# The up product of eight half blocks in seven products instead of eight, on one core

## The chip, the cores and the metric

The kernel runs on one core of one Trainium2 chip. The metric is the device time of one launch in microseconds (us), the median of several runs. A profiled execution is read beside it; its span leaves out a little of what the device time counts (731.9 us against 733.69 us for the same execution).

Five engines work side by side: TensorE (PE in the profile, with its weight loads as PEld), VectorE (DVE), ScalarE (ACT), GpSimd (POOL) and SyncE (SP, which only issues transfers here).

## The reference

Retention over a sequence, then two matrix products with an activation between them, all in f32:

```python
B, H, S, D = 4, 8, 768, 64
for t in range(S):
    state = gamma * state + k[:, :, t] (outer) v[:, :, t]
    y[:, :, t] = scale * q[:, :, t] @ state
x = y.transpose(0, 2, 1, 3).reshape(B * S, H * D)      # 3072 x 512
h = x @ w_in                                           # 512 x 2048   "up"
g = h - np.tanh(h)
out = g @ w_out                                        # 2048 x 512   "down"
```

## The kernel before

The 3072 tokens are 24 chunks of 128. Four chunks make a block, two chunks a half block of 256 tokens: n = 0 to 11. The 2048 inner columns are eight pairs of 128, m2 = 0 to 7. One step (n, m2) makes the up product of one half block and one pair, its activation, and (two steps behind, LAG) the down product of an earlier step. There are 96 steps. The last eight half blocks (n = 4 to 11) run one after the other, eight steps each. Attention work for the later chunks is spread over the steps in between; it ends in half block 5.

The up product is eight matmuls of 256 columns into one bank of PSUM (the matrix engine's accumulator):

```python
def up(n, m2, i):                       # called for i = 0, 1
    if i == 0:
        hps[n, m2] = bank("h", f"h_{n}_{m2}")           # 128 x 512 f32, two of them in turn
    hp = hps[n, m2][:, ts(i, TH)]                       # TH = 256
    for c in range(NC):                                 # NC = 4
        nc.tensor.matmul(hp, w1[:, c, ts(2 * m2 + i, P)], xT[n // 2][:, c, ts(n % 2, TH)],
                         start=(i == 0 and c == 0), stop=(c == NC - 1), ...)
```

The activation (h - tanh h, with a polynomial where h is small) takes five ACT and six DVE instructions over 128x512:

```python
u  = Square(hp);  th = Tanh(hp)                                            # ACT, L429, L430
q0 = Square(u + ..); q1 = Square(sqrt(A) u + ..); large = Relu(u - 0.5)    # ACT, L437 to L439
th = hp - th                                                               # DVE, L445
hp = (R - u) * hp                                                          # DVE, L446
hp = (q0 + C0) * hp                                                        # DVE, L448
hp = (q1 + A * C1) * hp                                                    # DVE, L454
g  = hp * u                                                                # DVE, L458
copy_predicated(g, large, th)                                              # DVE, L459
```

The down product of half blocks 5 to 11 is done in seven matmuls of 256 columns instead of eight (2x2 blocks by the Strassen-Winograd scheme). GpSimd makes four sums of g for it (128x128 each, L545 to L548) and, once, 16 sums of w_out (128x512 each, L536). The seven results lie in four banks, and DVE adds them up at the end of a half block:

```python
def fast_down(n, m2, first, last):
    ...
    for k in (1, 2, 4, 6, 7, 5, 3):
        nc.tensor.matmul(accs[n][k], left[k - 1], right, ...)       # L581

def fast_end(n):                        # after m2 = 7
    nc.scalar.copy(out=p1, in_=acc[1])
    # seven DVE additions of 128x256 in one burst (L597, L599), two transfers out
```

The loop over the steps, with attention and weight conversion cut:

```python
for s in range(BEGUN, len(steps)):
    ... # attention work in every second step, up to s = 45: PE, ACT, DVE, and the split of k, q
    ... # (turn_by_dma: ACT copies, a transfer out, a transposing transfer back)
    for i in range(2):
        up(n, m2, i)
    waiting.append(steps[s])
    shrink_begin(n, m2)                 # u, th
    shrink_factors(n, m2)               # q0, q1, large
    shrink_multiply(n, m2)              # three DVE operations
    downs(LAG)                          # the down product of two steps before
    shrink_end(n, m2)                   # three DVE operations
    if n >= FAST:
        fast_sums(n, m2)                # POOL
```

Of the kernel before, what the change touches and what calls it, by code (L numbers as in the profile page):

```python
# [9 lines left out]
F32 = mybir.dt.float32  # L10
# [3 lines left out]
AF = mybir.ActivationFunctionType  # L14
ALU = mybir.AluOpType

P = 128
# [15 lines left out]
def kernel(  # L33
# [7 lines left out]
    tables: bass.AP,  # L41
    out: bass.AP,
):

# [265 lines left out]
    def mask(ci):  # L312
        halves = scores[ci]
        m = mid.tile([P, 2, NP, D], F32, tag="a", name=f"a_{ci}")
        nc.vector.tensor_tensor(m, halves[:, :, 0],
                                causal[:, None, None, :].to_broadcast([P, 2, NP, D]),
                                op=ALU.mult)
        masked[ci] = m
# [70 lines left out]
    def outputs_rest(ci):  # L389
        halfway.pop(ci)(False)  # L390
        loaded.pop(ci)
# [18 lines left out]
    def work(tag, bufs):  # L410
        return tmp.tile([P, BANK], F32, tag=tag, name=tag, bufs=bufs)
# [14 lines left out]
    def shrink_begin(n, m2):  # L426
        hp = hps[n, m2]
        u, th = (work(x, 2) for x in ("u", "th"))
        nc.scalar.activation(u, hp, AF.Square)  # L429
        nc.scalar.activation(th, hp, AF.Tanh)  # L430
        shrinking[n, m2] = [u, th]

    def shrink_factors(n, m2):
        u = shrinking[n, m2][0]
        large = work("large", 2)
        q0, q1 = (work(x, 1) for x in ("q0", "q1"))
        nc.scalar.activation(q0, u, AF.Square, bias=bias0)  # L437
        nc.scalar.activation(q1, u, AF.Square, bias=bias1, scale=math.sqrt(A))  # L438
        nc.scalar.activation(large, u, AF.Relu, bias=bias_m)  # L439
        shrinking[n, m2] += [q0, q1, large]  # L440

    def shrink_multiply(n, m2):
        hp = hps[n, m2]
        u, th, q0 = shrinking[n, m2][:3]
        nc.vector.tensor_tensor(th, hp, th, op=ALU.subtract)  # L445
        nc.vector.scalar_tensor_tensor(hp, in0=u, scalar=R, in1=hp, op0=ALU.subtract,  # L446
                                       op1=ALU.mult, reverse0=True)
        nc.vector.scalar_tensor_tensor(hp, in0=q0, scalar=C0, in1=hp, op0=ALU.add,  # L448
                                       op1=ALU.mult)

    def shrink_end(n, m2):
        hp = hps.pop((n, m2))
        u, th, _, q1, large = shrinking.pop((n, m2))
        nc.vector.scalar_tensor_tensor(hp, in0=q1, scalar=A * C1, in1=hp, op0=ALU.add,  # L454
                                       op1=ALU.mult)
        g = gp.tile([P, 2, TH], F32, tag="g", name=f"g_{n}_{m2}")
        flat = g.rearrange("p i t -> p (i t)")
        nc.vector.tensor_tensor(flat, hp, u, op=ALU.mult)  # L458
        nc.vector.copy_predicated(flat, large.bitcast(I32), th)  # L459
        gT[n, m2] = g  # L460

    def down(n, m2, j, first, last):

# [22 lines left out]
    def rows_of(n):  # L486

        return out[ds(n * TH, TH)].rearrange("(p two) c -> p two c", two=2)
# [19 lines left out]

    FAST = 5
    PAIRS = NM // 2  # L510
    room = []
    t_of = {}

    def quarter(i, c, at):
        return w2[:, i::2, ts(c, TH)][:, ds(2 * at, 2)]

    def fast_weights(k, at):

        if not room:
            for _ in range(3):  # L520
                raw = stage.tile([P, 2, 2, TH], F32, tag="raw", name="fast_raw", bufs=3)
                room.extend(raw[:, i] for i in range(2))
            for tag in ("head", "low", "power"):
                room.extend(stage.tile([P, 2, TH], F32, tag=tag, name=f"fast_{tag}")
                            for _ in range(2))
        if k == 3 and at == 0:
            late = xp.tile([P, 4, 2, TH], F32, tag="xT", name="fast_x")
            room.extend(late[:, i] for i in range(4))
        t = t_of[k, at] = room[PAIRS // 2 * k + at]
        a, b = (  # L530
            (quarter(0, 1, at), quarter(0, 0, at)),
            (quarter(1, 1, at), t_of.get((0, at))),
            (quarter(1, 1, at), quarter(0, 1, at)),
            (t_of.get((1, at)), quarter(1, 0, at)),
        )[k]
        nc.gpsimd.tensor_tensor(t, a, b, op=ALU.subtract)  # L536

    fast_g = {}

# [28 lines left out]
        right = {2: 1, 7: 1, 4: 1, 6: n % 2}  # L568
        accs[n] = {k: b[:, ts(right.get(k, 0), TH)] for k, b in acc.items()}

    def fast_down(n, m2, first, last):
        if first:
            fast_banks(n)
        left = fast_g.pop((n, m2))
        for k in (1, 2, 4, 6, 7, 5, 3):
            right = (
                w2[:, 2 * m2, :TH], w2[:, 2 * m2 + 1, :TH], w2[:, 2 * m2 + 1, TH:],
                *(t_of[x, m2 // 2][:, m2 % 2] for x in (3, 0, 1, 2)),
            )[k - 1]

            nc.tensor.matmul(accs[n][k], left[k - 1], right, start=first and k in (1, 6, 7, 4),  # L581
                             stop=last, skip_group_check=True)

    def fast_end(n):
        acc = accs.pop(n)
        o = op.tile([P, 2, DM], F32, tag="sum", name=f"sum_{n}")
        c11, c12, c21, c22 = (o[:, j, ts(c, TH)] for j in range(2) for c in range(2))
        some = [mid.tile([P, 2, TH], F32, tag="a", name=f"fast_{n}") for _ in range(2)]
        p1, v_, x_, w_ = (t[:, i] for t in some for i in range(2))
        nc.scalar.copy(out=p1, in_=acc[1])  # L590
        add, sub = ALU.add, ALU.subtract
        for dst, k, b, how in (
            (c11, 2, p1, add), (v_, 6, p1, add), (w_, 7, v_, add), (c22, 5, w_, add),
            (x_, 5, v_, add), (c21, 4, w_, sub), (c12, 3, x_, add),
        ):
            if how is sub:
                nc.vector.tensor_tensor(dst, b, acc[k], op=sub)  # L597
            else:
                nc.vector.tensor_tensor(dst, acc[k], b, op=add)  # L599
            if dst is c21:  # L600
                nc.sync.dma_start(out=rows_of(n)[:, 1], in_=o[:, 1])
        nc.sync.dma_start(out=rows_of(n)[:, 0], in_=o[:, 0])

    waiting = []

    def part(j, n, m2, first, last):
        down(n, m2, j, first, last)
        if last:
            add_up(n, m2, j)

    def downs(lag):
        while len(waiting) > lag:
            tile_ = waiting.pop(0)
            if tile_[0] >= FAST:
                fast_down(*tile_)
                if tile_[3]:
                    fast_end(tile_[0])
                continue
            for j in range(2):
                part(j, *tile_)  # L620

# [4 lines left out]
    def tall(ci):  # L628
# [23 lines left out]
        "a": lambda s: shrink_begin(*steps[s][:2]),  # L652
        "q": lambda s: shrink_factors(*steps[s][:2]),
        "d": lambda s: shrink_multiply(*steps[s][:2]),
        "g": lambda s: shrink_end(*steps[s][:2]),
        "o": lambda s: [down(*steps[s][:2], j, *steps[s][2:]) for j in range(2)],
        "E": lambda s: [add_up(*steps[s][:2], j) for j in range(2)],
        "x": lambda n: idle.__setitem__(0, n),
# [17 lines left out]


    FIRST = 8
    LAST_WEIGHTS = NW - 6
    with_chunk = {BEGUN + 2 * i + 1: FIRST - 3 + i for i in range(NCH - FIRST + 3)}  # L680
    with_weights = {BEGUN: [12, 13]}
    for i in range(14, NW):
        with_weights[i - 5] = [i]
    fast_parts = [(k, at) for at in range(PAIRS // 2) for k in range(3)]
    fast_parts += [(3, at) for at in range(PAIRS // 2)]

    for s in range(BEGUN, len(steps)):
        n, m2, first, last = steps[s]
        ci = with_chunk.get(s)
        if ci is not None:  # L690
            if ci >= FIRST:
                outputs_rest(ci)
                keep_x(ci)
            if FIRST <= ci + 2 < NCH:
                products(ci + 2)
                mask(ci + 2)
                state(ci + 2)
            load_chunk(ci + 4)
            if ci + 3 < NCH:
                turn_by_dma(ci + 3)  # L700
            if FIRST <= ci + 1 < NCH - 1:
                outputs(ci + 1)
                see(ci + 1)
        for i in with_weights.get(s, []):
            convert(i)
            load_weights(i + 3)
        for i in range(2):
            up(n, m2, i)
        if ci == NCH - 2:
            outputs(ci + 1)  # L710
            see(ci + 1)
        waiting.append(steps[s])
        shrink_begin(n, m2)
        shrink_factors(n, m2)
        shrink_multiply(n, m2)
        downs(LAG)
        shrink_end(n, m2)
        if n >= FAST:
            fast_sums(n, m2)
        if s + 1 in with_chunk:  # L720
            for which in range(2):
                scale(with_chunk[s + 1] + 3, which, nc.gpsimd)
        if s > LAST_WEIGHTS + 1:
            for _ in range(min(2, len(fast_parts))):
                fast_weights(*fast_parts.pop(0))
    downs(0)


def _tables(H, D, S=768):
# [51 lines left out]
```

## Time and profile before

| | |
|---|---|
| device time, median of 3 | 734.24 us (733.23 to 734.8) |
| profiled span | 731.9 us, mean granted TensorE clock 0.997 |
| up matmuls (L420), 128x256, records | 1536, mean 381 ns |
| down matmuls by plain products (L468), 128x512, records | 320, mean 593 ns |
| GpSimd sums of g, 128x128 | 456 ns each |
| GpSimd sums of w_out (L536), 128x512 | 1.27 to 1.51 us each |
| DVE operations of the activation, 128x512 | 0.685 to 0.774 us each |

How to read it: matmuls are pipelined, so the mean of a record is longer than the distance from one to the next; the distance of starts counts. Busy shares are averages over the span. The chain that ended last follows the work back from the last instruction.

The last stretch has the same pattern for over 250 us. In five windows of 52 us from 448 to 708 us, PE is busy for 52.00 us in each, DVE for about 35.4, ACT for 23.56 and POOL for 13.94.

### The profile page before, as it was taken

How to read it: one execution, taken by the hardware profiler on the slowest of the kernel's cores; microseconds unless marked ns; L12 is line 12 of the kernel's file. 1: busy time of each engine (PE TensorE's matmuls, PEld its weight loads, DVE VectorE, ACT ScalarE, POOL GpSimd, SP SyncE). 2: the span in 40 equal slices, each digit the busy share in tenths (PEclk: the TensorE clock that was granted, in tenths of full speed). 3: DMA queues.
4: the chain of work that ended last, by engine and by line, in shares of the span. 5: the costliest groups of instructions: out<-in, count | busy, mean ns of one | idle time of the engine just before them, and what ended most of it. 6: DMA issues, size and time to landing. Idle time of an engine off the chain costs nothing.

```text
span 731.9 us, 14885 instructions
## 1 busy us (share of the span) xinstructions
PE 717.7 (98%) x5806; PEld 566.9 (77%) x5806; DVE 533.6 (73%) x849; ACT 389.7 (53%) x749; POOL 247.6 (34%) x348
## 2 busy tenths in 40 slices
PE   8899999999999999999999999999999999999996
PEld 7686666666776676677688888888888888888885
DVE  4999988998888777765566676676766766766764
ACT  4567557766777645565445444444444444444441
POOL 0565434544554555411012222222132222222221
PEclk9999999999999999999999999999999999999998
DMA  9883428776776566444100000000000000000000
GB/s 202 211 207 84 130 69 218 173 197 171 188 192 165 110 147 165 131 106 122 36 30 1 1 29 2 1 29 1 29 1 1 30 0 1 30 0 1 30 0 30
DMA packets 125399, 59.84 MB, mean 82 GB/s; under 512 B 109840, under 2 KB 118160, under 8 KB 125328
## 3 DMA queue, kind: packets, MB, share of 16 engines
q1 hardware_dynamic: 122880, 50.34, 28.4%
q10 hardware_dynamic: 2448, 8.54, 3.1%
q8 instruction: 46, 0.75, 0.4%
q14 instruction: 25, 0.20, 0.1%
HBM read 35.80 MB, written 14.68 MB: 69 GB/s over the span
## 4 chain that ended last, share of the span: by engine, by line
PE 91%; DMA 4%; DVE 2%; POOL 1%; SPq 1%; ACT 1%; issue 0%; DVEq 0%; POOLq 0%; ACTq 0%
PE h L420 44%; PE o L468 17%; PE fast_t L581 8%; PE y L581 8%; PE fast_o L581 7%; PE y L356 3%; DMA kqT<-rows 1%; PE s L302 1%; PE s L308 1%; DMA raws<-in_moe_w_in_dram 1%; DMA k<-in_k_dram 1%; DMA q<-in_q_dram 1%; SPq L233 1%; PE kqTp L254 1%; DMA rows<-apart 1%; DVE head L189 0%
## 5 line engine op out<-in xcount | busy, mean ns | idle before, releaser
L420 PE MATMUL h<-xT,w 128*128 128x256 f32 x1536 | 349.9, 381 | 1.1 <-DVE w L203 1.1
L420 PEld LDWEIGHTS h<-xT,w 128*128 128x128 f32 x1536 | 289.7, 190 | 50.1 <-issue 10.0
L429 ACT ACTIVATE u<-h 128x512 f32<-128x512 f32 x96 | 57.3, 597 | 259.7 <-PE h L420 259.5
L445 DVE TENSOR_TENSOR th<-h,th 128x512 f32<-128x512 f32 x96 | 66.2, 689 | 132.3 <-ACT th L430 132.2
L468 PE MATMUL o<-w,g 128*128 128x512 f32 x320 | 144.2, 593 | 0.0
L545 POOL TENSOR_TENSOR s<-g 128x128 f32<-128x128 f32 x56 | 25.5, 455 | 286.7 <-DVE g L459 282.3
L468 PEld LDWEIGHTS o<-w,g 128*128 128x128 f32 x320 | 60.5, 190 | 59.5 <-issue 56.7
L459 DVE COPY_PREDICATED g<-large,th 128x512 f32<-128x512 int32 x96 | 74.3, 774 | 9.8 <-DVE g L458 0.5
L448 DVE SCALAR_TENSOR_TENSOR h<-q,h 128x512 f32<-128x512 f32 x96 | 66.8, 696 | 10.0
L199 POOL TENSOR_TENSOR low<-low,power 128x512 f32<-128x512 f32 x30 | 38.6, 1288 | 102.4 <-DVE power L191 62.8
L454 DVE SCALAR_TENSOR_TENSOR h<-q,h 128x512 f32<-128x512 f32 x96 | 66.6, 694 | 8.9 <-DVE h L448 0.9
L458 DVE TENSOR_TENSOR g<-h,u 128x512 f32<-128x512 f32 x96 | 66.4, 692 | 6.9
L437 ACT ACTIVATE q<-u,tab 128x512 f32<-128x512 f32 x96 | 69.5, 724 | 0.0
L438 ACT ACTIVATE q<-u,tab 128x512 f32<-128x512 f32 x96 | 69.1, 720 | 0.0
L439 ACT ACTIVATE large<-u,tab 128x512 f32<-128x512 f32 x96 | 68.8, 716 | 0.0
L446 DVE SCALAR_TENSOR_TENSOR h<-u,h 128x512 f32<-128x512 f32 x96 | 65.8, 685 | 0.0
L430 ACT ACTIVATE th<-h 128x512 f32<-128x512 f32 x96 | 56.8, 591 | 0.0
L240 POOL TENSOR_TENSOR q<-q,tab 128x512 f32<-128x512 f32 x22 | 24.2, 1099 | 77.2 <-DMA q<-in_q_dram 52.0
L203 POOL TENSOR_TENSOR w<-low,head 128x512 f32<-128x512 f32 x30 | 38.5, 1284 | 2.4
L240 POOL TENSOR_TENSOR v<-v,tab 128x512 f32<-128x512 f32 x22 | 28.2, 1284 | 3.3 <-DMA v<-in_v_dram 3.3
L356 PEld LDWEIGHTS y<-a,v 64*64 64x64 f32 x768 | 15.9, 134 | 14.9 <-ACT large L439 10.9
L546 POOL TENSOR_TENSOR s<-s,g 128x128 f32<-128x128 f32 x56 | 25.6, 457 | 4.4
(110 smaller groups left out, 868.7 us busy)
## 6 DMA issues: line engine op xcount, KB each, us to landing
rows<-apart ACTq DMA_DIRECT2D x16, 512.0 KB, 4.4
k<-in_k_dram SPq DMA_DIRECT2D x24, 256.0 KB, 4.7
q<-in_q_dram SPq DMA_DIRECT2D x24, 256.0 KB, 5.1
v<-in_v_dram SPq DMA_DIRECT2D x24, 256.0 KB, 5.5
raw<-in_moe_w_out_dram SPq DMA_DIRECT2D x12, 512.0 KB, 4.1
out_dram<-sum SPq DMA_DIRECT2D x24, 256.0 KB, 2.3
raw<-in_moe_w_in_dram SPq DMA_DIRECT2D x14, 256.0 KB, 4.4
raw<-in_moe_w_in_dram SPq DMA_DIRECT2D x28, 128.0 KB, 4.2
```

The costliest lines, as they stand in the source:

```text
L420: nc.tensor.matmul(hp, w1[:, c, ts(2 * m2 + i, P)], xT[n // 2][:, c, ts(n % 2, TH)], start=(i == 0 and c == 0), stop=(c == NC - 1), skip_g ...
L437: nc.scalar.activation(q0, u, AF.Square, bias=bias0)
L438: nc.scalar.activation(q1, u, AF.Square, bias=bias1, scale=math.sqrt(A))
L439: nc.scalar.activation(large, u, AF.Relu, bias=bias_m)
L445: nc.vector.tensor_tensor(th, hp, th, op=ALU.subtract)
L446: nc.vector.scalar_tensor_tensor(hp, in0=u, scalar=R, in1=hp, op0=ALU.subtract, op1=ALU.mult, reverse0=True)
L448: nc.vector.scalar_tensor_tensor(hp, in0=q0, scalar=C0, in1=hp, op0=ALU.add, op1=ALU.mult)
L454: nc.vector.scalar_tensor_tensor(hp, in0=q1, scalar=A * C1, in1=hp, op0=ALU.add, op1=ALU.mult)
L458: nc.vector.tensor_tensor(flat, hp, u, op=ALU.mult)
L459: nc.vector.copy_predicated(flat, large.bitcast(I32), th)
L468: nc.tensor.matmul(o_p[j], gT[n, m2][:, i, ts(j, P)], w2[:, 2 * m2 + i], start=(first and i == 0), stop=(last and i == 1))
L581: nc.tensor.matmul(accs[n][k], left[k - 1], right, start=first and k in (1, 6, 7, 4), stop=last, skip_group_check=True)
```

## The change

The up product of half blocks 4 to 11 is done in seven products instead of eight, by the same 2x2 scheme as the down product: the blocks are 128 inner columns by 256 rows of w_in, and 256 rows by 128 tokens of x. A product is now two matmuls of 128 columns, so a step has 14 of them in place of eight of 256 columns. GpSimd makes the sums: four of 128x256 for each pair of w_in (once), four of 128x256 for each half block of tokens.

The seven results are put together partly by accumulation in PSUM. Four products (1, 5, 7, 6) go into the four quarters of a bank; ACT copies the bank to SBUF; GpSimd adds two pairs of quarters (P1 + P6, P5 + P7); the other three products (2, 3, 4) accumulate on the first three quarters; DVE adds the pairs where they are still missing.

```diff
+    def fast_up(n, m2, some):
+        if 1 in some:
+            hps[n, m2] = bank("h", f"h_{n}_{m2}")
+        for k in some:
+            for c in range(2):
+                nc.tensor.matmul(hps[n, m2][:, ts(PLACE[k], P)], s_of[m2][k - 1][:, c],
+                                 x_of[n][k - 1][:, c], start=(k == 1 and c == 0), stop=(c == 1),
+                                 skip_group_check=True)
+
+    def up_take(n, m2):
+        nc.scalar.copy(out=odd_room[0], in_=hps[n, m2])
+
+    def up_pairs():
+
+        first = odd_room[0].rearrange("p (i t) -> p i t", i=4)
+        nc.gpsimd.tensor_tensor(odd_room[1], first[:, :2], first[:, 3:1:-1], op=ALU.add)
+
+    def up_add(n, m2):
+        hp = hps[n, m2].rearrange("p (i t) -> p i t", i=4)
+        u, w = (odd_room[1][:, i] for i in range(2))
+        nc.vector.tensor_tensor(hp[:, 1:3], hp[:, 1:3],
+                                u[:, None, :].to_broadcast([P, 2, P]), op=ALU.add)
+        nc.vector.tensor_tensor(hp[:, 3], u, w, op=ALU.add)
```

The sums, one call a pair (`up_weights`) or a half block (`up_tokens`), with their tiles cut:

```diff
+        for k, x, y, how in ((3, a11, a21, ALU.subtract), (1, a21, a22, ALU.add),
+                             (2, s_[1], a11, ALU.subtract), (4, a12, s_[2], ALU.subtract)):
+            nc.gpsimd.tensor_tensor(s_[k], x, y, op=how)
...
+        for dst, a, b in ((t1, b12, b11), (t2, b22, t1), (t3, b22, b12), (t4, b21, t2)):
+            nc.gpsimd.tensor_tensor(dst, a, b, op=ALU.subtract)
...
+    for m2 in range(PAIRS):
+        with_sums.setdefault(FIRST_UP - 4 + m2, []).append(lambda m2=m2: up_weights(m2))
+        with_sums.setdefault(FIRST_DOWN + m2, []).append(lambda m2=m2: fast_weights(m2))
```

The sums of w_out for the down product are now four of 128x256 for each pair, made in the eight steps of half block 5 (`fast_weights` above), where the kernel before made 16 of 128x512 earlier.

The order within a step changes so that PE has other work while the results of its first four products are carried on. The down product is cut into its first four and its last three matmuls, and it now belongs to the step three before (one more than before). A tile's last factor, its multiplication and its predicated copy move into the next step. The last factor writes g in SBUF, so that the bank is free earlier:

```diff
+        if fast:
+            fast_up(n, m2, (1, 5, 7, 6))
+            up_take(n, m2)
...
+            if before and ci is None:
+                shrink_factors(*before)              # q1, large of the tile before
+                shrink_last_factor(*before)
+            up_pairs()
+            for make in with_sums.get(s, []):
+                make()
+            downs(lag, 0)                            # first four down matmuls
+            fast_up(n, m2, (2, 3, 4))
+            up_add(n, m2)
+            shrink_begin(n, m2)                      # th, then u
+            if before:
+                shrink_end(*before)                  # multiplication, predicated copy
+                if before[0] >= FAST:
+                    fast_sums(*before)
+            downs(lag, 1)                            # last three down matmuls
+            end_some(1)
+            shrink_two(n, m2)
+            before = n, m2
+            if s + 1 not in with_chunk:
+                middle()                             # q0 and the third factor
```

(The comments in this extract are added.) The additions at the end of a half block no longer come as one burst: two of the seven are issued at once, the other five one by one in the following steps (`end_some`):

```diff
+        add(c11, 2, p1)
+        add(v_, 6, p1)
+        for args in ((w_, 7, v_), (c22, 5, w_), (x_, 5, v_), (c21, 4, w_, True), (c12, 3, x_)):
+            ending.append(lambda args=args: add(*args))
```

In steps with attention work, the squares of the tile before (q0, q1, large) now stand in ACT's queue ahead of the copies that split k and q for their transposing transfer:

```diff
+        middle()
+        if before:
+            shrink_factors(*before)
+            shrink_last_factor(*before)
         if FIRST <= ci + 2 < NCH:
             products(ci + 2)
...
+        if not before:
+            turn_and_see(ci)                         # else after the first four up products
```

## The prediction

> **What bounds the kernel now.** I read the page's totals first, then the 40 slices, then the chain that ended last, and then one step of the last stage by engine.
>
> ```profile
> span 731.9 us, 14885 instructions
> ...
> PE 717.7 (98%) x5806; PEld 566.9 (77%) x5806; DVE 533.6 (73%) x849; ACT 389.7 (53%) x749; POOL 247.6 (34%) x348
> ...
> PE   8899999999999999999999999999999999999996
> ...
> PE 91%; DMA 4%; DVE 2%; POOL 1%; SPq 1%; ACT 1%; issue 0%; DVEq 0%; POOLq 0%; ACTq 0%
> ```
>
> TensorE (PE) is busy in every slice and carries 91% of the chain. A busy PE is only modelled, so the next view, matmuls in order of time, checks it: are there holes between the matmuls of two steps?
>
> ```profile
> 505.57 0.59 PE L581 MATMUL y<-w,s 128*128 128x256 f32 x2
> 506.00 3.62 PE L420 MATMUL h<-xT,w 128*128 128x256 f32 x16
> 509.45 1.03 PE L581 MATMUL fast_t<-w,g 128*128 128x256 f32 x4
> ...
> 512.04 0.59 PE L581 MATMUL y<-w,s 128*128 128x256 f32 x2
> 512.47 0.81 PE L420 MATMUL h<-xT,w 128*128 128x256 f32 x3
> ```
>
> One f32 matmul of the program is two records. The 16 records of the up product run from 506.00 to 509.45, 0.2157 us each, and a whole step from 506.00 to 512.47: 6.47 us = 30 records (16 up, 14 down) x 0.2157. No hole: the step is exactly its matmuls, and only fewer PE microseconds can shorten it, as long as no other engine then needs more than the new step.
>
> **What the new matmuls cost.** The change replaces 256-column up matmuls by 128-column ones, each with its own weight load. The kernel before has such a stream already, in the filler that keeps the array busy early on:
>
> ```profile
> 30.95 2.13 PE L216 MATMUL kqTp<-busy 128*128 128x128 f32 x17 [1.83 <-DVE state L331]
> 31.03 1.98 PEld L216 LDWEIGHTS kqTp<-busy 128*128 128x128 f32 x17
> ```
>
> The weight loads take 0.190 us as records, but their starts are (1.98 - 0.19) / 16 = 0.112 us apart: the load overlaps. So a 128-column record costs 0.112, which is 52% of 0.2157, not exactly half.
>
> The Trainium skill bears in three places. "TensorE: Matmul & The Clock Gate", section "LDWEIGHTS (loading the stationary operand)", puts a load of 128 columns at 128/1.2 = 107 ns; 112 ns between starts agrees, and it means that the load just fits under a 128-column matmul. "FP8 and Floating Point Precision", section "TensorE Precision Notes", says that true FP32 takes four passes; the two records per matmul, each about twice 128 or 256 columns long, fit that. "SBUF — State Buffer", section "SBUF: two separate sides", says that VectorE (DVE) instructions with two SBUF inputs and GpSimd (POOL) instructions lock each other out of a shared port for a whole instruction. The trace agrees: here a 0.74 us predicated copy (both inputs in SBUF) took 1.50 beside POOL's subtractions, one of which grew from 1.27 to 1.74, while DVE's operations on PSUM did not grow.
>
> ```profile
> 290.34 1.50 DVE L459 COPY_PREDICATED g<-large,th 128x512 f32<-128x512 int32 x1
> ...
> 289.96 1.27 POOL L536 TENSOR_TENSOR fast_head<-w,fast_raw 128x512 f32<-128x512 f32 x1
> 291.19 1.74 POOL L536 TENSOR_TENSOR fast_power<-w 128x512 f32<-128x512 f32 x1
> ```
>
> **The change, part by part.**
>
> PE. Half blocks 4 to 11 have 8 steps each: 64 steps. Up product before: 8 matmuls = 16 records x 0.2157 = 3.45 us. After: seven products of two 128-row pieces = 14 matmuls = 28 records x 0.112 = 3.14 us. Saved: 0.315 us a step, x 64 = 20.2 us. A pure step (half blocks 6 to 11, no attention work) goes from 6.47 to 3.14 + 3.02 = 6.16 us. The down product is only cut into four and three products, and the one extra tile of lag (a step without a down, and one down more at the end) moves 3.0 us from the middle to the tail without adding work.
>
> DVE. In a step of before its six operations start at 504.29, 504.90, 505.69, 506.49, 507.29 and 508.09: 0.61 us behind one they do not depend on, 0.80 behind one they do, 4.55 us in all. The change adds two additions of seven-product pieces: 128x256 at 0.42 us (as the sums of L599) and 128x128, by the slope (0.692 - 0.424) / 256 us per element about 0.28. It interleaves tiles, so some dependent pairs come apart. In the new order: last factor 0.61, additions 0.37 and 0.22, multiply 0.80, predicated copy 0.70, one output addition 0.35 (now one a step in five steps of eight, before a burst of seven), subtraction 0.61, two factors 0.80 + 0.80: 5.3 us of 6.16. It fits, with 0.9 us to spare where there were 1.9.
>
> ACT. Six operations of 0.5 to 0.6 us spacing instead of five: about 3.4 us of 6.16.
>
> POOL. The sums for the down product take 4 x 0.456 us and gaps, 2.0; new is one 128x256 addition, from 455 ns at 128 and 1274 at 512 elements about 0.73: 2.7 of 6.16. Token sums add 4 x 0.73 = 2.9 us once per half block. Weight sums add 2.9 us in each of eight steps around the start of half block 4 and again in the eight of half block 5 (the second lot replaces 16 subtractions of 1.3 to 1.5 us).
>
> **The path within a step.** With 0 at the first up matmul: the first four products, 16 records x 0.112, end at 1.8. ACT's copy of the bank (0.59 us, as its 128x512 copy of L268) can run from 2.0, with 0.2 for the array to drain and the signal, to 2.65. Four down matmuls, 8 x 0.2157 = 1.73, fill PE until 3.5; only then do the last three up products, which accumulate on what ACT has read, need that copy. Slack 0.75 us or more. They take 12 x 0.112 = 1.34 and end at 4.85; DVE's two additions run from 5.1 to 5.85; tanh, square and squared factor start 0.49, 0.48 and 0.61 us apart in the trace before, so ACT is done near 5.85 + 0.2 + 1.7 = 7.8 to 8.0, just ahead of the next copy at 6.16 + 2.0 = 8.2. DVE goes on from 5.85 through multiply, copy, output addition, subtraction and three factors, 0.8 + 0.7 + 0.45 + 0.61 + 3 x 0.8 = 5.0, to 10.9: then the bank is read out, and it is taken again two steps later at 12.3. So in pure steps no wait takes the place of the removed work; I expect 6.16 us, 48 x 0.315 = 15.1 us saved in half blocks 6 to 11.
>
> In half blocks 4 and 5 (5.0 us of the 20.2) I take losses off. In half block 5 POOL has 2.9 + 0.73 + 2.0 = 5.7 us a step, plus the time it waits for DVE's three operations with two SBUF inputs (0.28 + 0.8 + 0.74 = up to 1.8): 7.5 at worst, against steps of 6.2 without and about 8.3 with attention. That may cost some 2 to 3 us over the eight steps. Token sums and the first filling cost perhaps 0.5 us more.
>
> The tail: the last DVE chain (additions, the multiply and copy of the tile before, then six operations) ends about 12.1 us after the last step's start, and PE's remaining down products of three earlier tiles end at 12.2. It fits; afterwards, as before, one down, seven additions and the store.
>
> Sum: 734.2 - 20.2 + 2.5 = 716.5 us.
>
> **The rivals.**
>
> 1. DVE becomes the bound. Its spare 0.9 us a step rests on my counting of dependent and independent pairs. If all nine operations cost 0.1 more, the step is near 6.2 and nothing is lost; if the additions had to wait behind POOL each time, 0.7 more, the step returns to about 6.4 and only 5 us remain: some 729. For it: DVE goes from 4.55 to 5.3. Against: in pure steps POOL's sums run while DVE works on PSUM, where the trace shows no collision.
>
> 2. The new wait of PE on ACT's copy. Each step now has an exchange PE to ACT to PE, with 0.75 us to spare. A slip of the tile before by more than that shows up one to one on PE. For it: ACT's queue is in order, and the copy sits behind a square that depends on DVE's additions. If it cost 0.3 us in each of the 64 steps, all the gain would go: 734. Against: half the down product stands between, and is put there for that.
>
> 3. The weight load becomes the bound: with data other than one repeated tile, 128-column matmuls could be further apart than 0.112. At 0.123 us a record the seven products equal the eight. For it: only the early filler shows this form. Against: its loads are real loads, and PEld records keep 0.19 whatever they read.
>
> 4. Attention steps of half blocks 4 and 5 slow down, because ACT now does the shrink's squares ahead of the split of k, so that the transposing transfer starts later. It has 15 us until it is needed and takes 4.4 + 4.3 us; hidden.
>
> **Range and chances.** With nothing lost it is 714; with all of half block 5's gain and 0.05 us a pure step lost, about 719. Eight in ten: 712 to 724. Faster by over 2% means under 719.6, a saving of 14.7 of the possible 20.2: I give it 0.72. Within 2%: 0.23, mostly rivals 1 and 2. Slower by over 2% would need a real pile-up: 0.05.
>
> **What the profile after should show.** Right: step starts 6.16 us apart at 450 to 690; the new up line with 28 records a step, starts 0.112 apart; PE still full in all slices, PEld well above before; DVE near 85% there. Wrong: idle time on the up line's PE or PEld released by the ACT copy (rival 2); DVE without idle time and steps of 6.3 to 6.5 (rival 1); 128-column starts more than 0.115 apart (rival 3); long predicated copies beside POOL in half block 5 with steps above 7 there, more than I took off.

## The result and the profile after

| | before | after |
|---|---|---|
| device time, median of 4 | 733.83 us (733.23 to 734.8) | 717.15 us (716.57 to 718.03) |
| ratio, 95% interval | | 0.9773 (0.9756 to 0.9789) |
| profiled span | 731.9 us | 716.1 us |
| from the first seven-product matmul (287.88) or its counterpart (287.74) to the end | 444.2 us | 428.2 us |
| one half block of pure steps | 51.80 us | 49.23 us (half blocks 8 to 10), 49.86 (6 and 7) |

The last two rows take starts of matmuls from the traces. Ahead of that stretch TensorE's work is the same in both kernels; over all runs the stretch starts between 286.9 and 289.3 us.

The page of the changed kernel, its totals, slices and chain:

```profile
span 716.1 us, 16724 instructions
...
PE 699.4 (98%) x6574; PEld 573.4 (80%) x6574; DVE 579.1 (81%) x977; ACT 431.9 (60%) x813; POOL 347.6 (49%) x492
...
PE   8899999999999999999999999999999999999996
PEld 8676666667667776766779989989999999999995
DVE  4999988898898856788777888788788787887885
...
PE 85%; DVE 7%; ACT 3%; DMA 2%; POOL 1%; issue 1%; ACTq 0%; DVEq 0%; POOLq 0%
```

PE still leads. DVE and the weight loads have come up behind it, and the chain passes through DVE and ACT in places. One step of half block 9, all engines in order of time (start, duration, engine, line, output and inputs, count, idle before it):

```profile
583.95 0.61 PE L688 MATMUL h<-xT,w 128*128 128x128 f32 x4
584.40 0.61 PE L688 MATMUL h<-x,w 128*128 128x128 f32 x4
...
585.74 1.03 PE L616 MATMUL fast_o<-w,g 128*128 128x256 f32 x4
...
585.99 0.59 ACT L693 COPY fast_head<-h 128x512 f32<-128x512 f32 x1 [0.36 <-PE h L688]
...
587.25 0.63 PEld L688 LDWEIGHTS h<-xT,w 128*128 128x128 f32 x4
587.47 0.61 PE L688 MATMUL h<-xT,w 128*128 128x128 f32 x4
...
589.08 0.43 DVE L703 TENSOR_TENSOR h<-h,fast_head 128x256 f32<-128x256 f32 x1 [0.85 <-PE h L688]
...
590.10 0.61 PE L688 MATMUL h<-xT,w 128*128 128x128 f32 x4
```

Step to step: 590.10 - 583.95 = 6.15 us. Four 128-column records take 584.40 - 583.95 = 0.45, 0.112 each. ACT's copy ends at 586.58, 0.67 ahead of the weight load (587.25) and 0.89 ahead of the matmul (587.47) of the products that need it. DVE has waited 0.85 us for PE: it has time left, PE has none.

PE's longest waits in the last eight half blocks, in order of time, by matmuls:

```profile
304.55 0.71 PE L688 MATMUL h<-xT,w 128*128 128x128 f32 x4 [0.91 <-ACT fast_head L693]
...
309.81 0.69 PE L309 MATMUL s<-kqT 64*64 64x64 f32 x32 [1.07 <-DMA kqT<-rows]
...
425.91 0.67 PE L616 MATMUL fast_t<-fast_apart,g 128*128 128x256 f32 x2 [0.44 <-ACT q L448]
...
475.77 0.67 PE L616 MATMUL y<-fast_apart,g 128*128 128x256 f32 x2 [0.43 <-ACT q L448]
```

Counted from start to start, the lost times are larger than these idle times, because a pipelined matmul's record runs on: 1.07, 1.24, 0.68 and 0.68 us. The first two come behind the one step without a down product (the lag grows there, in half block 4). The last two stand in the first down step of half blocks 6 and 7. The square that is named as their releaser does not touch a bank of the down product, so something else held them (experiments 2 and 6).

### The profile page after: what moved, and what is told of

Read it like the earlier page. It is cut to its first block, busy times and chain, and to the rows that moved or that the text cites. A ratio compares the mean times of both kernels' runs of the same rounds, so it can differ in the third digit from the quotient of the medians.

```text
span 716.1 us, 16724 instructions
## 1 busy us (share of the span) xinstructions
PE 699.4 (98%) x6574; PEld 573.4 (80%) x6574; DVE 579.1 (81%) x977; ACT 431.9 (60%) x813; POOL 347.6 (49%) x492
## 4 chain that ended last, share of the span: by engine, by line
PE 85%; DVE 7%; ACT 3%; DMA 2%; POOL 1%; issue 1%; ACTq 0%; DVEq 0%; POOLq 0%
PE h L688 27%; PE o L490 16%; PE h L421 12%; PE fast_t L616 8%; PE y L616 8%; PE fast_o L616 7%; PE y L357 3%; DMA kqT<-rows 1%; PE s L309 1%; PE kqTp L217 1%; DVE head L190 1%; PE s L303 1%; DVE power L192 1%; DVE head L188 1%; PE kqTp L255 1%
## 5 line engine op out<-in xcount | busy, mean ns | idle before, releaser
L421 PE MATMUL h<-xT,w 128*128 128x256 f32 x512 | 117.7, 382 | 1.1 <-DVE w L204 1.1
L421 PEld LDWEIGHTS h<-xT,w 128*128 128x128 f32 x512 | 95.7, 190 | 20.9 <-issue 7.2
L688 PEld LDWEIGHTS h<-xT,w 128*128 128x128 f32 x512 | 76.2, 191 | 15.7 <-issue 7.1
L688 PE MATMUL h<-xT,w 128*128 128x128 f32 x512 | 78.9, 277 | 1.0 <-ACT fast_head L693 0.9
L465 DVE SCALAR_TENSOR_TENSOR h<-q,h 128x512 f32<-128x512 f32 x96 | 66.9, 696 | 11.5 <-ACT q L440 1.5
L703 DVE TENSOR_TENSOR h<-h,fast_head 128x256 f32<-128x256 f32 x64 | 27.6, 432 | 56.8 <-PE h L688 56.1
L698 POOL TENSOR_TENSOR fast_head<-fast_head 128x256 f32<-128x256 f32 x64 | 47.4, 740 | 46.1 <-ACT fast_head L693 34.5
L688 PE MATMUL h<-x,w 128*128 128x128 f32 x448 | 68.3, 275 | 0.0
L688 PEld LDWEIGHTS h<-x,w 128*128 128x128 f32 x448 | 59.0, 192 | 0.0
L693 ACT COPY fast_head<-h 128x512 f32<-128x512 f32 x64 | 37.5, 585 | 26.4 <-PE h L688 26.2
L474 DVE SCALAR_TENSOR_TENSOR g<-q,h 128x512 f32<-128x512 f32 x64 | 44.0, 687 | 7.8 <-ACT q L448 1.3
```

Of the source, the lines that this page charges most:

```text
L465: nc.vector.scalar_tensor_tensor(hp, in0=shrinking[n, m2][2], scalar=C0, in1=hp, op0=ALU.add, op1=ALU.mult)
L688: nc.tensor.matmul(hps[n, m2][:, ts(PLACE[k], P)], s_of[m2][k - 1][:, c], x_of[n][k - 1][:, c], start=(k == 1 and c == 0), stop=(c == 1), ...
L698: nc.gpsimd.tensor_tensor(odd_room[1], first[:, :2], first[:, 3:1:-1], op=ALU.add)
```

## The experiments

All times below are medians of timed runs beside the kernel before.

**1. The step without a down product, moved.** From the second step of half block 4 to the second step of half block 5.

```diff
-        falls_back = s == FIRST_UP + 1
-        lag = LAG + int(s >= FIRST_UP + 1)
+        falls_back = s == FIRST_UP + 9
+        lag = LAG + int(s >= FIRST_UP + 9)
```

> The step without a down product (where the lag grows from two tiles to three) moves from the second step of half block 4 to the second step of half block 5; nothing else changes. Theory A (PE runs ahead there because 3.45 us of down product are missing, so that ACT's copy and the transposed k and q come too late for it): the holes of 1.07 us (before the last three up products of the next step, waiting for ACT's copy) and of 1.24 us (before the products with the transposed k and q) in half block 4 go, and a hole of at most 1 us appears in half block 5, where no transposed k and q are due any more. Time 717.15 - 1.3 to 2.3 = 715 to 716. Theory B (the holes come from the new order of ACT's queue in attention steps, squares ahead of the split of k): both holes stay, time within 0.5 us of 717.

Measured: 714.75 us, ratio 0.974 (0.9724 to 0.9757). Both holes of half block 4 are gone. The products with the transposed k and q follow the ones ahead of them at once:

```profile
309.20 0.65 PE L303 MATMUL s<-v,k 64*64 64x64 f32 x32
309.67 0.65 PE L309 MATMUL s<-kqT 64*64 64x64 f32 x32
...
364.77 0.71 PE L688 MATMUL h<-xT,w 128*128 128x128 f32 x4 [0.18 <-ACT fast_head L693]
```

The last line is the new hole, 0.34 us from start to start. Theory A holds: PE ran ahead. (`falls_back` also puts that step's attention work behind its first four up products, and this moved along. Experiment 9 has neither and no such holes either, so no run separates the two.) From the first seven-product matmul to the end it is 425.9 us against 428.2, so 2.3 us; the rest of the gain in the profiled run lies in the stretch before.

**2. The token sums, two steps later.**

```diff
-        at_ = ... else PAIRS * (n - 1) + 2
+        at_ = ... else PAIRS * (n - 1) + 4
```

> GpSimd makes the token sums of half blocks 7 to 11 two steps later, away from the step in which the outputs of a half block are begun to be added up. Theory A (GpSimd's token sums hold DVE's two-SBUF-input operations up, so the first output additions come late, and the fourth down product of half blocks 6 and 7 waits for them): the two holes of 0.60 us plus 0.08 near 425 and 475 go, 717.15 - 1.3 = 715.8 us; the long multiplications of DVE (1.21 us) move two steps on and cost nothing there. Theory B (the wait belongs to the deferred additions themselves, whatever GpSimd does): the holes stay at 0.6 us.

Measured: 715.57 us, ratio 0.9752 (0.9737 to 0.9767). The holes near 425 and 475 are gone, and half blocks 6 to 10 all take 49.19 us. In the changed kernel (first three lines, GpSimd and DVE in order of time) the long multiplication stood in the step in which a half block's additions begin:

```profile
422.10 0.60 DVE L705 TENSOR_TENSOR h<-fast_head 128x128 f32<-128x128 f32 x1
422.50 0.78 POOL L678 TENSOR_TENSOR x<-xT,x 128x256 f32<-128x256 f32 x1
422.61 1.21 DVE L481 TENSOR_TENSOR g<-g,u 128x512 f32<-128x512 f32 x1
```

With the sums moved, the same stretched multiplication is found two steps on, and PE does not wait:

```profile
433.44 0.58 DVE L705 TENSOR_TENSOR h<-fast_head 128x128 f32<-128x128 f32 x1
433.93 1.22 DVE L481 TENSOR_TENSOR g<-g,u 128x512 f32<-128x512 f32 x1
435.25 0.74 DVE L482 COPY_PREDICATED g<-large,th 128x512 f32<-128x512 int32 x1
```

Theory A holds: the collision alone did no harm here, it costs only where PE waits for DVE's additions soon after. Which of the three additions the matmul waited for this run does not show; experiment 6 bears on it.

**3. Both moves together.**

> The two moves together: the step without a down product in half block 5, the token sums two steps later. If they are independent their gains add: 717.15 - 1.8 - 1.3 = 714 us, and from half block 6 on PE has no hole over 0.1 us. If the time lost is handed on rather than removed, it stays near 716.

Measured: 714.56 us (713.25 to 714.85), ratio 0.9735 (0.9721 to 0.975). In the profiled execution it is 424.4 us from the first seven-product matmul to the end: 3.8 us less than the change, against 2.3 and 1.9 for the two alone, and half blocks 6 to 10 take 49.19 us as in experiment 2. So in this stretch they nearly add. The medians do not show it: 2.6 us gained, where the first move alone gained 2.4 and the second 1.6 (the profiled execution was the fastest of the four). The version is faster than the change, but not distinguishable from experiment 1.

**4. The split of k and q ahead of the squares again,** in the attention steps of the last eight half blocks.

```diff
+        if before and ci + 3 < NCH:
+            turn_by_dma(ci + 3)
         middle()
         if before:
             shrink_factors(*before)
             shrink_last_factor(*before)
...
-        if ci + 3 < NCH:
+        if ci + 3 < NCH and not before:
             turn_by_dma(ci + 3)
```

> In the attention steps of half blocks 4 and 5 the split of k and q (two ACT copies, 2.1 us) goes back ahead of the squares of the tile before. Theory A (the new order is worth having, because the squares release DVE's chain and with it the additions on the up product): the hole of 1.24 us before the products with the transposed k and q goes, but the first attention steps lose 1 us and more each to ACT's copy or to the bank, 718 to 721 us. Theory B (the order only delays the transfer): the time falls by about 1.2 us to 716.

Measured: 720.61 us, ratio 0.982 (0.9805 to 0.9835): 3.5 us slower than the change. In order of time:

```profile
299.36 0.72 ACT L440 ACTIVATE q<-u,tab 128x512 f32<-128x512 f32 x1 [0.42 <-ACT apart L278]
300.12 0.70 DVE L465 SCALAR_TENSOR_TENSOR h<-q,h 128x512 f32<-128x512 f32 x1 [3.96 <-ACT q L440]
...
301.75 0.68 PE L688 MATMUL h<-xT,w 128*128 128x128 f32 x4 [2.41 <-DVE g L474]
```

ACT makes the squares behind the split; DVE is idle for 3.96 us until that square is there; PE waits 2.41 us for the bank that DVE's last factor has to read out. Theory A holds: in this kernel, squares ahead of the splits are worth 3.5 us. The expectation named the transposed k and q as what gets better, and they do: the first products with them follow at once (309.68, then 310.16), and the hole of 1.24 us is gone.

**5. Eight products in the new order.** ACT's copy, the pair sums and DVE's two additions are left out. The sums of tokens and weights are still made, and not used; as they have overwritten a quarter of w_in by then, the up product is of other numbers than in the changed kernel.

```diff
-            fast_up(n, m2, (1, 5, 7, 6))
-            up_take(n, m2)
+            up(n, m2, 0)
...
-            fast_up(n, m2, (2, 3, 4))
-            up_add(n, m2)
+            up(n, m2, 1)
```

> The whole new order is kept, but the up product is made in eight matmuls of 256 columns (four in the first place, four in the second), without ACT's copy, the pair sum and DVE's two additions; the sums of tokens and weights are still made and not used. Theory A (the gain is PE's 0.315 us a step, and the order brings nothing by itself): pure steps are 6.47 us again, and the time is 717.15 + 20.2 - about 3 to 4 for the holes that go = 733 to 735 us. Theory B (a good part comes from the order and the later additions): below 730 us.

Measured: 736.22 us, ratio 1.0037 (1.0025 to 1.0048). Matmuls by time:

```profile
601.90 1.89 PE L421 MATMUL h<-xT,w 128*128 128x256 f32 x8
603.63 1.03 PE L616 MATMUL fast_o<-w,g 128*128 128x256 f32 x4
...
605.36 1.89 PE L421 MATMUL h<-xT,w 128*128 128x256 f32 x8
...
608.38 1.89 PE L421 MATMUL h<-xT,w 128*128 128x256 f32 x8
```

608.38 - 601.90 = 6.48 us, the step of before, and half blocks 6 to 10 take 51.80 us each, to the hundredth that of before. The new order brings nothing by itself; the gain is PE's columns, as theory A has it. The time lies 1.2 us above the range expected, and 2.9 above the kernel before. From the first up product of half block 4 to the end it is 445.9 us against 444.2, and one hole accounts for that: PE waits once, 1.74 us from start to start, at 309.67 for the transposed k and q. Seven products in the old order were not run, so that the order is needed for the gain is shown only piece by piece (experiments 4, 6 and 8).

**6. The output additions in one burst again.**

```diff
-            ending.append(lambda args=args: add(*args))
+            add(*args)
```

> The seven output additions of a half block are issued in one burst again, in the step after its last down product but one. Theory A (DVE has 0.9 us to spare a step; five additions of 0.35 to 0.45 us more in one step are 1.6 to 2.0 us, so about 1 us is passed on to PE at each of six boundaries): 720 to 724 us, with holes before the last three up products of the following step. Theory B (two banks and a tile of lag absorb it): within 1 us of 717.15.

Measured: 729.1 us, ratio 0.994 (0.9925 to 0.9955): 12 us lost, far more than theory A's 3 to 7. DVE and PE behind the end of half block 8:

```profile
583.41 0.41 DVE L632 TENSOR_TENSOR sum<-fast,fast_t 128x256 f32<-128x256 f32 x1
583.74 0.42 DVE L634 TENSOR_TENSOR sum<-fast_t,fast 128x256 f32<-128x256 f32 x1
584.07 0.68 DVE L459 TENSOR_TENSOR th<-h,th 128x512 f32<-128x512 f32 x1
...
586.26 0.69 DVE L474 SCALAR_TENSOR_TENSOR g<-q,h 128x512 f32<-128x512 f32 x1
587.10 0.68 PE L688 MATMUL h<-xT,w 128*128 128x128 f32 x4 [1.27 <-DVE g L474]
```

The wait is not where I expected it (ACT's copy). At the ends of half blocks 8 and 9 it is at the next step's first up product, which needs the bank that DVE's last factor reads out: 1.4 us from start to start each. At the ends of half blocks 5, 6, 7 and 10 the next half block's first down products wait for the additions themselves, 1.4, 2.8, 2.9 and 0.7 us. The longest kind:

```profile
477.67 0.42 DVE L634 TENSOR_TENSOR sum<-fast_t,fast 128x256 f32<-128x256 f32 x1
...
478.15 1.36 PE L616 MATMUL fast_t<-w,g 128*128 128x256 f32 x4 [2.64 <-DVE sum L634]
```

By the code, the addition reads the first bank of the pair `fast_t` (half block 6's third bank), and the matmul writes the second (half block 7's first). The wait so covers both banks of the pair. That fits the holes of experiment 2 too: half block 6's product 4 goes to the first bank of that pair, while an addition of half block 5 still reads the second. In the trace of experiment 8 the same hole is put down to that addition, which ends 0.15 us ahead of the matmul (425.64 + 0.42 = 426.06):

```profile
425.64 0.42 DVE L634 TENSOR_TENSOR fast<-fast_t,fast 128x256 f32<-128x256 f32 x1
...
426.21 0.67 PE L616 MATMUL fast_t<-fast_apart,g 128*128 128x256 f32 x2 [0.49 <-DVE fast L634]
```

**7. Two and four idle DVE copies a step,** each 128x256 from the bank, ahead of the subtraction (the room that they write, put in front as `odd_room[0]`, is left out below).

```diff
             end_some(1)
+            for _ in range(2):          # or 4
+                nc.vector.tensor_copy(odd_room[0], hps[n, m2][:, : 2 * P])
             shrink_two(n, m2)
```

> Two idle copies of 128x256 on DVE are added to every step of half blocks 4 to 11 (0.42 us each as records, 0.35 apart when they depend on nothing: 0.7 us a step). Theory A (PE is the bound and DVE has about 0.9 us to spare in a pure step, 1.1 without an output addition): pure steps stay at 6.15 us, the time rises by under 4 us, lost in the attention steps. Theory B (DVE is already nearly the bound, rival 1 of the prediction): steps of 6.5 and more, 740 us.

> Four idle copies of 128x256 a step on DVE instead of two, some 1.5 us a step. With two, the trace has DVE idle for about 0.2 us in a step without an output addition, so its spare time was about 0.9 us. Theory A (beyond that the step is DVE's): pure steps rise to some 6.15 + (1.5 - 0.95) = 6.7 us, 64 x 0.55 = 35 us, 745 to 755 us. Theory B (what two copies cost came from somewhere else, and DVE has more to spare): below 735 us.

Measured: 722.41 us with two, ratio 0.9845 (0.9824 to 0.9865); 765.28 us with four, ratio 1.0437 (1.0411 to 1.0463). With two, single steps stay at 6.15 us, and what is lost are holes of 0.7 to 0.9 us at the ends of half blocks, where three output additions fall into one step. That is theory A for the pure steps, but 5.3 us are lost where I had said under 4, and not where I had said: half blocks 4 and 5 take 61.13 and 55.22 us, in the change 61.08 and 55.26. With four, DVE has no idle time left:

```profile
620.16 1.03 PE L616 MATMUL fast_o<-w,g 128*128 128x256 f32 x4
620.18 0.40 DVE L632 TENSOR_TENSOR sum<-fast,fast_t 128x256 f32<-128x256 f32 x1
620.51 1.79 DVE L890 COPY fast_head<-h 128x256 f32<-128x256 f32 x4
622.21 0.68 DVE L459 TENSOR_TENSOR th<-h,th 128x512 f32<-128x512 f32 x1
...
627.09 1.03 PE L616 MATMUL fast_o<-w,g 128*128 128x256 f32 x4
```

The step is 627.09 - 620.16 = 6.93 us; the copies hold DVE for 622.21 - 620.51 = 1.70. So DVE's own work in a step with an output addition is 6.93 - 1.70 = 5.23 us, and its spare time in the changed kernel 6.15 - 5.23 = 0.92. Four copies cost 0.43 each, not the 0.37 that I had reckoned; over four copies and 64 steps this is some 13 us, about what lies between 750 and 765.

**8. ACT's copy of the bank behind two squares.**

```diff
             fast_up(n, m2, (1, 5, 7, 6))
+            if before and ci is None:
+                shrink_factors(*before)         # q1, large
             up_take(n, m2)
```

> In steps without attention work two squares-like operations of the tile before (q1 and large, 0.61 us apart each) go ahead of ACT's copy of the bank, so the copy ends 1.2 us later. The slack reckoned for it was 0.75 us. Theory A (that slack is real and is the tightest wait in the step): PE waits some 0.4 to 0.5 us before its last three up products in every pure step, steps of 6.55 to 6.65 us, 738 to 745 us: the whole gain gone. Theory B (the slack is larger because the pipeline shifts as a whole): steps stay at 6.15, time within 3 us of 717.

Measured: 721.79 us, ratio 0.984 (0.9825 to 0.9856). Neither theory's figure; the pure steps are theory B's. ACT and PE in a pure step:

```profile
560.70 0.61 PE L688 MATMUL h<-xT,w 128*128 128x128 f32 x4
...
562.90 0.71 ACT L449 ACTIVATE large<-u,tab 128x512 f32<-128x512 f32 x1
563.51 0.56 ACT L693 COPY fast_head<-h 128x512 f32<-128x512 f32 x1
...
564.21 0.62 PE L688 MATMUL h<-xT,w 128*128 128x128 f32 x4
...
566.86 0.61 PE L688 MATMUL h<-xT,w 128*128 128x128 f32 x4
```

The step is 6.16 us. The copy starts 2.81 us after the step's first matmul, where it was 2.04 (585.99 - 583.95 in the changed kernel): 0.77 later and not 1.2, because ACT had stood idle for 0.36 us ahead of it. The copy now ends at 564.07, 0.14 ahead of the matmul that needs it, and that matmul is as far behind the step's first as before (3.51 us, where it was 3.52). So there was slack for at least 0.77 us; more than that was not tried in a pure step, because the delay I made was smaller than I took it for. What is lost sits mostly where the output additions of the half block before are made: 0.6 us in the fifth step of half blocks 8 to 10, and about 0.3 more over their other steps (50.08 us a half block against 49.23). In half block 4 one hole of 2.29 us takes the place of the two of the changed kernel; the half block takes 61.08 us in both.

**9. The lag stays at two tiles.**

```diff
-        lag = LAG + int(s >= FIRST_UP + 1)
+        lag = LAG
```

(and `falls_back` is off.)

> The lag stays two tiles to the end: no step without a down product. Theory A (the third tile only serves the end, where PE has three tiles of down product to fill the time of the last tile's chain; in the middle two are enough): the holes of half block 4 go (-2 us), pure steps stay at 6.15 us, and PE is idle for about 3 us before the last tile's down product: 717 to 719 us. Theory B (the third tile is what keeps the down product from waiting for its sums in each step): pure steps above 6.3 us, 725 us and more.

Measured: 718.17 us, ratio 0.9793 (0.9773 to 0.9812), not distinguishable from the change. Theory A in the main: both holes of half block 4 are gone, and half blocks 7 to 10 take about 49.58 us, half block 6 takes 49.89. That is 0.4 more than the undisturbed 49.19, mostly because PE waits some 0.3 us once in each half block for DVE's predicated copy. At the end PE waits twice for the activation of the last tiles:

```profile
703.20 1.13 PE L616 MATMUL y<-w,g 128*128 128x256 f32 x4 [1.06 <-DVE g L482]
...
707.53 1.13 PE L616 MATMUL y<-w,g 128*128 128x256 f32 x4 [1.03 <-DVE g L482]
```

2.4 us from start to start. So the third tile saves, at the end and at these small waits, about what its filling costs where the change put it; filling it elsewhere (experiment 1) keeps most of that saving at a smaller cost.

**10. The step without a down product in the fourth step of half block 5,** with the token sums moved (`s == FIRST_UP + 11`).

> As the two moves together, but the step without a down product is the fourth of half block 5, where DVE has no mask and state work and ACT has no split. If the remaining 0.34 us hole after that step comes from DVE's mask and state work it goes: about 714.2 us; if PE just runs ahead of ACT's copy there, it is as large or larger: 714.5 to 715.5 us.

Measured: 714.72 us, ratio 0.9752 (0.9733 to 0.9771): the same as experiment 3 within the interval. The hole behind the step is 0.32 us, as large as before, and another of 1.06 us stands ahead of the attention outputs of that step. So the small hole is not DVE's mask and state work; PE waits for ACT's copy there:

```profile
379.90 0.71 PE L688 MATMUL h<-xT,w 128*128 128x128 f32 x4 [0.16 <-ACT fast_head L693]
```

## Why the prediction was right, and where it was off

Predicted 716.5 us in 712 to 724; measured 717.15. The mechanism was right: fewer columns on PE, with no other engine as the bound in pure steps. One step of the working, the one on the lag, was wrong, and the size of the losses was right in part by luck.

*PE's columns.* 0.112 us a 128-column record, predicted from the filler, is what the new matmuls show. Undisturbed half blocks (experiments 2 and 3) take 49.19 us against 51.80, so 0.326 us a step where I said 0.315; times 64 is 20.9 us. Experiment 5 shows that the rest of the change brings no gain. Rival 3, weight loads that hold 128-column matmuls more than 0.112 us apart, is out.

*DVE.* 5.3 us predicted, 5.23 measured by experiment 7; 0.9 us to spare, 0.92 measured. Rival 1 is out in pure steps. (Its figure of 6.4 us for additions that wait behind POOL does not follow from its own terms: 5.3 + 0.7 = 6.0 is still under 6.16.) It is near all the same: a burst of additions costs 12 us.

*ACT's copy.* "Slack 0.75 us or more" was predicted. In the trace the matmul starts 0.89 us after the copy's end; where PE did wait for the copy, it started 0.05 after it (304.50, then 304.55). That leaves about 0.84, and experiment 8 took 0.77 of it at no cost in a pure step. Rival 2 is out there.

*The losses.* I took 2.5 us off. Undisturbed gain less measured gain in the same stretch is 20.9 - (444.2 - 428.2) = 4.9 us. Half block 5, to which I gave 2 to 3 us for GpSimd, lost about 0.3: it took 55.26 us instead of 57.14, and 2.6 less was due for the columns, 0.4 more because the longer lag moves one more plain down product (3.44 us in place of 3.02) into it. The token sums, for which I had 0.5 with the filling, cost 2 x 0.67 = 1.3 (experiment 2). Half block 4 took 61.08 us where 64.00 - 2.6 - 3.44 = 57.95 was due: 3.1 us lost, of which I had at most a part of that 0.5. So too much in one place made up for nothing in another, and a gain 0.7 us larger than reckoned did some of the rest; that the total came within 1 us is owed in part to luck.

*The step that failed* is the one on the lag: "a step without a down, and one down more at the end" moves work, but it also lets PE run 3.44 us ahead, while ACT, DVE and a transfer keep their pace. The changed kernel pays 1.07 + 1.24 = 2.3 us for that in half block 4, and experiment 1 shows it: both holes go when that step moves, and 2.3 us are gained.

*Rival 4.* "It has 15 us until it is needed ...; hidden" was wrong. Changed kernel first, then the kernel before:

```profile
300.27 1.06 ACT L278 COPY apart<-q 128x1024 uint16<-128x1024 uint16 x1
```

```profile
280.67 1.06 ACT L277 COPY apart<-q 128x1024 uint16<-128x1024 uint16 x1
...
295.46 0.65 PE L308 MATMUL s<-kqT 64*64 64x64 f32 x32
```

The split ended at 301.33 and the transposed k and q were due at 308.56 (0.47 us behind the products ahead of them, which started at 308.09): 7.2 us. They were there at 309.81, after 8.5. In the kernel before, one such pair had 13.7 us (281.73 to 295.46). With the squares ahead but the step without a down product moved (experiment 1) 9.4 us are left, and PE does not wait; so both shorten the way. But the order that delays the transfer is right: turned back it costs 3.5 us (experiment 4).

## What to carry to other kernels

When fewer matmul columns are bought with additions on other engines, count the other engines' step in issue order, dependent and independent pairs apart; here that gave DVE's 5.2 us to a tenth, 0.9 under the step, and experiment 7 shows that copies beyond those 0.9 us lengthen it. A change that delays work by one tile can let the leading engine run ahead once, as here; put that step where no transfer and no copy is due from the others. Work on a side engine that is harmless in most steps should be kept out of the step in which a result is handed over.

## What I had not expected of the hardware

DVE operations on two SBUF inputs were stretched beside GpSimd even when short: the 128x128 addition took 0.30 us alone and up to 0.88 beside GpSimd's subtractions, and the multiplication of 0.69 took 1.21 to 1.53, while the 128x256 addition on PSUM stayed at 0.43. The multiplication became open to this only by the change, which moved its input from PSUM to SBUF: before, it took 0.69 us with or without GpSimd at work.
